# A spectral mixing layer and a feed-forward part on one Trainium2 core: turns of the interleaved transform from 6 to 5.5 half steps, and the short form of `w_out` from two tiles sooner

## The chip, the cores and the metric

The kernel runs on one core of one Trainium2 chip. The metric is the device time of one launch in microseconds (us); before the change its median is 2561.6 us. The engines are named as in the profile: PE (matrix products; PEld its weight loads), DVE (vector engine), ACT (scalar engine), POOL (GpSimd), SP (here only a queue that issues transfers).

## The reference

```python
def _attn_ref(x, w_r, w_i, b_r, b_i):              # x: 8 x 3008 x 256
    X = np.fft.rfft(x, axis=1)
    Yr = X.real @ w_r - X.imag @ w_i + b_r
    Yi = X.real @ w_i + X.imag @ w_r + b_i
    Yr = np.sign(Yr) * np.maximum(np.abs(Yr) - 0.01, 0.0)      # Yi likewise
    return np.fft.irfft(Yr + 1j * Yi, n=x.shape[1], axis=1)

def _moe_ref(x, w_in, w_out):                      # x: 24064 x 256, d_ff 2048
    r = np.maximum(x @ w_in, 0.0)
    return (r * r) @ w_out
```

The second function is applied to the output of the first. All is float32.

## The kernel before, in words

**Two streams of work.** The transform of a batch (forward stages, a complex mix with soft shrinkage, backward stages) is split into many small jobs. The feed-forward part goes over 48 tiles of tokens, six for each of the 8 batches, 504 or 500 tokens wide, each seen as two halves of h = 252 or 250 columns (the first two tiles of a batch have 252, the other four 250). A tile has 8 steps `n`, one for each 256 of the 2048 hidden units. A step has two half steps.

**A step on PE.** `Step.first` issues 12 products `psh` with `w_in`, `Step.second` the other 9: the 2x2 block product is done by seven block products instead of eight, each in three terms (high x high, low x high, high x low) that together keep float32 accuracy from fp32r operands. The operands are the tile's tokens and five sums of them (`Tokens`: B11, B21, B22, T1, T3, T2, T4), each in a high half `yt0` (an ACT cast) and a low half `yt1` (a POOL subtraction). The fourth product of a step, `S2 T2`, needs `T2`, which is made of the last columns of the tile. DVE adds the products up and rectifies them into `mc`; ACT squares `mc` and casts it to the high half `mg0`; POOL subtracts to get the low half `mg1`. Two steps later `Step.out` issues 12 matmuls `pso` of 2h columns with `w_out`.

**The short form.** In the steps `SEVEN = (1, 2, 4, 5)` of the tiles in `FREE` (line 61, tiles 38 to 46), `out_seven` (lines 809 to 832) does `w_out` by seven block products as well: 21 matmuls of h columns in place of 12 of 2h. It needs four sums of weight blocks (`out_sums`, made once when the transform is over and its memory free), and on the side of the data `cast_early` (788 to 793: the fourth block's halves `mh`, `ml`) and `forms` (795 to 807: sums `ftt` on DVE, high halves `fth` on ACT, low halves `ftl` on POOL). Its extra accumulators are joined per tile by `tile_sums` on DVE.

**What sets the order.** The main loop (1155 to 1187) goes over half steps; before each half step ends it calls the jobs whose time in half steps has come. The transform of batch b+1 is cut in 13 turns of `PACE` = 6 half steps (lines 60, 898 to 909, 1133 to 1141). Each tile's columns come from two or three inverse transforms `Back` (`back_tasks`, 911 to 935), which are loaded through one buffer `du`, transformed on PE with `dx` in groups of three matmuls into `psf`, copied by ACT (`dy`) and added by DVE into `yr`; then `Tokens.sums` (POOL `ms`) and `Tokens.split` follow. For the last two batches all inverse transforms are made ahead, in `kept_tasks` (948 to 960), once the last batch's mixing is done: two at a time are loaded (`load_two`), and their results `dy` go to memory. They begin at half step `done + 0.6`, where `done` is where the last pairs end, and tiles 36 and on read their tokens back (`raw_load`). Within these calls the framework fixes the order of each engine's instructions when the kernel is built; on the chip every engine follows its list in order, and SP issues its transfers in order.

**The tiles in FREE** take their tokens one piece at a time at steps 0, 6 and 7 (`Tokens.free`), put between the casts, so that POOL's list is written out by hand there.

## Time and profile before

| | us |
|---|---|
| median of 3 runs (2561.59 to 2561.8) | 2561.6 |
| the profiled execution | 2562.7 |
| its span | 2560.9 |
| PE busy | 2551.0 |
| DVE busy | 1875.5 |
| POOL busy | 1782.0 |
| ACT busy | 1452.5 |

The span is the time from the first to the last instruction in the trace; the profiled execution's own time is 1.8 us longer and 1.1 us above the median. PE's granted clock is 1.00 of full speed all over. An engine's busy time counts neither its waits nor the issuing of transfers. In the order of the run: a front part to about 160 us, the turns to about 1950 us, the kept transforms to about 2145 us (the start of tile 38), and from there the short steps.

### The profile page before, as it was taken

To read this page: it belongs to the slowest core of one execution; us is meant where nothing else is said; L and a number is where in the kernel's file an instruction comes from. 1 tells how busy PE (TensorE), PEld (TensorE's weight loads), DVE (VectorE), ACT (ScalarE), POOL (GpSimd) and SP (SyncE) were. 2 spreads that over 40 slices of the span, in tenths; PEclk is the share of its full clock that TensorE was granted. 3 is DMA by queue.
4 is the path that set the end of the run, shared out by engine and by line. 5 is a ranking of instruction groups with operands and counts; after the bars stand their busy time and mean duration, and the time that the engine had idled before them with its cause. 6 is when DMAs were issued, how large, how long until landed. Compare 5 with 4: busy or idle time off the path is not lost.

```text
span 2560.9 us, 48190 instructions
## 1 busy us (share of the span) xinstructions
PE 2551.0 (100%) x17534; PEld 2365.2 (92%) x17534; DVE 1875.5 (73%) x3714; ACT 1452.5 (57%) x2338; POOL 1782.0 (70%) x1804
## 2 busy tenths in 40 slices
PE   9999999999999999999999999999999999999999
PEld 7899999999999999999999999999999999999998
DVE  7876776777777777777677777777776656888885
ACT  5655555555555555555555555555555555666664
POOL 1167666776767777666676766766566857999995
PEclk9999999999999999999999999999999999999999
DMA  9633432333334333343333343332333452101000
GB/s 312 196 94 92 115 93 85 95 111 106 104 108 119 106 102 97 116 121 112 92 104 112 106 122 100 108 112 89 108 111 95 126 151 62 33 21 33 13 17 17
DMA packets 191203, 257.05 MB, mean 100 GB/s; under 512 B 18216, under 2 KB 138016, under 8 KB 190968
## 3 DMA queue, kind: packets, MB, share of 16 engines
q1 hardware_dynamic: 177553, 228.71, 28.9%
q0 software_dynamic: 13280, 25.16, 4.1%
q8 instruction: 140, 2.29, 0.4%
q14 instruction: 95, 0.78, 0.1%
q10 hardware_dynamic: 135, 0.12, 0.0%
HBM read 150.36 MB, written 103.55 MB: 99 GB/s over the span
## 4 chain that ended last, share of the span: by engine, by line
PE 97%; DVE 1%; DMA 1%; POOL 0%; ACT 0%; issue 0%; SPq 0%; DVEq 0%; ACTq 0%
PE pso L594 38%; PE psh L594 36%; PE psf L312 7%; PE psf L291 3%; PE psf L345 2%; PE psf L253 2%; PE psf L594 2%; PE psf L477 1%; PE psf L558 1%; PE psf L559 1%; PE psf L555 1%; PE psf L375 1%; PE psf L532 1%; DMA x<-x_in 0%; PE psf L487 0%; PE psf L463 0%
## 5 line engine op out<-in xcount | busy, mean ns | idle before, releaser
L115 POOL TENSOR_TENSOR mg<-mc,mg 128x500 fp32r<-128x500 f32 (+3 forms) x766 | 967.6, 1285 | 386.7 <-ACT mg L111 295.4
L594 PE MATMUL pso<-mg,wout 128*128 128x500 f32 (+2 forms) x4284 | 1080.1, 388 | 0.0
L594 PE MATMUL psh<-yt,win 128*128 128x250 f32 (+1 forms) x8064 | 1073.4, 280 | 0.8 <-DVE mc L594 0.3
L594 PEld LDWEIGHTS psh<-yt,win 128*128 128x128 f32 x8064 | 1017.7, 189 | 27.0 <-DVE yt L115 0.6
L594 PEld LDWEIGHTS pso<-mg,wout 128*128 128x128 f32 x4284 | 766.4, 188 | 120.5
L594 DVE CUSTOM_DVE_ANT_0 mc<-psh,mv 128x250 f32<-128x250 f32 (+3 forms) x769 | 418.3, 546 | 282.5 <-PE psh L594 241.7
L594 ACT ACTIVATE mc<-mc 128x1000 f32<-128x1000 f32 (+4 forms) x420 | 407.9, 971 | 342.6 <-DVE mc L594 340.4
L111 ACT CAST mg<-mc 128x1000 fp32r<-128x1000 f32 (+2 forms) x385 | 381.8, 992 | 13.9
L594 DVE TENSOR_TENSOR mv<-psh,mu 128x500 f32<-128x500 f32 (+1 forms) x384 | 260.8, 679 | 47.2 <-PE psh L594 13.3
L312 PE MATMUL psf<-wx,kxh 128*128 128x256 f32 x1008 | 210.9, 281 | 0.0
L333 DVE TENSOR_TENSOR kv<-psf,ke 64x256 f32<-64x256 f32 x336 | 141.8, 422 | 56.1 <-PE psf L312 42.1
L312 PEld LDWEIGHTS psf<-wx,kxh 128*128 128x128 f32 x1008 | 167.5, 189 | 2.7 <-DVE ke L324 0.2
L111 ACT COPY dy<-psf 128x188 f32<-128x188 f32 (+2 forms) x229 | 70.8, 315 | 167.2 <-PE psf L559 166.7
L224 POOL TENSOR_TENSOR xs<-xt 120x256 f32<-120x256 f32 x156 | 120.7, 795 | 60.1 <-DMA xt<-x_in 21.1
L112 DVE COPY mp<-psh 128x250 f32<-128x250 f32 (+1 forms) x304 | 126.6, 416 | 46.5 <-PE psh L594 31.7
L115 POOL TENSOR_TENSOR ksl<-kv,ksh 128x512 fp32r<-128x512 f32 x84 | 109.8, 1307 | 66.6 <-ACT ksh L111 59.8
L312 PE MATMUL psf<-wx,kxl 128*128 128x256 f32 x504 | 141.5, 281 | 0.0
L594 DVE TENSOR_TENSOR mu<-psh,mp 128x250 f32<-128x250 f32 (+1 forms) x304 | 127.2, 418 | 9.5
L594 DVE CUSTOM_DVE_ANT_0 mc<-psh,mp 128x250 f32<-128x250 f32 (+1 forms) x304 | 124.2, 408 | 4.8 <-PE psh L594 4.7
L115 POOL TENSOR_TENSOR yt<-yr,yt 128x250 fp32r<-128x250 f32 (+1 forms) x94 | 88.6, 944 | 43.6 <-ACT yt L111 43.1
L115 POOL TENSOR_TENSOR ftl<-ftt,fth 128x250 fp32r<-128x250 f32 (+1 forms) x144 | 107.5, 772 | 7.3 <-ACT fth L111 2.5
L335 ACT ACTIVATE kc<-kv,low 128x512 f32<-128x512 f32 x84 | 60.8, 724 | 88.4 <-DVE kv L333 88.3
(182 smaller groups left out, 3311.1 us busy)
## 6 DMA issues: line engine op xcount, KB each, us to landing
ka<-s SPq DMA_DIRECT2D x96, 256.0 KB, 3.0
du<-s SPq DMA_DIRECT2D x86, 256.0 KB, 2.9
kcm<-cm_in POOLq DMA_DIRECT2D x84, 256.0 KB, 3.7
s<-kuh SPq DMA_DIRECT2D x84, 256.0 KB, 3.2
s<-kul SPq DMA_DIRECT2D x84, 256.0 KB, 3.7
s<-xe SPq DMA_DIRECT2D x82, 240.0 KB, 2.4
xt<-x_in SPq DMA_DIRECT2D x81, 240.0 KB, 3.2
out<-mo SPq DMA_DIRECT2D x64, 250.0 KB, 2.3
```

Of the source, the lines that this page charges most:

```text
L111: return act.copy(out=out, in_=in_)
L112: return eng.tensor_copy(out=out, in_=in_)
L115: return eng.tensor_tensor(out=out, in0=a, in1=b, op=ALU.subtract)
L224: return eng.tensor_tensor(out=out[:, :n], in0=self.xt[:, :n, 0], in1=self.xt[:, :n, 1], op=(ALU.add, ALU.subtract)[t])
L253: nc.tensor.matmul(ps[:, t], am_sb[0][:, j, t], v[:, t], start=n == 0, stop=n == 2)
L291: nc.tensor.matmul(pv[:, :, c, g, :], self.a[:, g, c * 128:(c + 1) * 128], bg, start=True, stop=True)
L312: self.last = nc.tensor.matmul(ps, l, wx[j][:, k, c, :], start=n == 0, stop=n == 5)
L333: dve.tensor_add(out=v[64 * r:64 * r + 64, g], in0=ps[gs], in1=self.e[gs, r])
L335: act.activation(r, v, AF.Relu, bias=low)
L345: nc.tensor.matmul(ps[:, g], self.cm[:, g, j * 128:(j + 1) * 128], r[:, g], start=n == 0, stop=n == 2)
L375: self.mm = nc.tensor.matmul(ps[:M1, t], nam if t and i else am32[:, t], self.xt[:, 0, i], start=i == 0, stop=i == 1)
L594: last_of[eng] = op(*args, **kwargs)
```

## The change

It does five things.

- `PACE` is 5.5, so the last pairs end and the kept transforms begin 33 half steps earlier: `done` goes from half step 554.25 to 521.25, from tile 34 to tile 32. The weight sums `out_sums` move with it.
- `FREE` is tiles 35 to 47; tile 35 has short steps 4 and 5, tile 47 steps 1, 2 and 4 (`SOME`), the others all four. That is 49 short steps in place of 36; the new ones are five with h = 250 (tiles 35, 47) and eight with h = 252 (tiles 36, 37).
- `cast_early` hands its POOL subtraction `ml` back, and `forms` issues it between its two halves.
- Tile 36 makes its tokens in the way of the tiles before, three half steps sooner, and reads its raw columns sooner.
- The last tile joins its short sums one step sooner, and its output leaves through DVE additions in place of ACT's copies and DVE's.

```diff
-TURN0, TURNS, PACE = 92, J, 6
-FREE = range(ENDS * len(HALF) + 2, B * len(HALF) - 1)
+TURN0, TURNS, PACE = 92, J, 5.5
+FREE = range(ENDS * len(HALF) - 1, B * len(HALF))
...
+SOME = {FREE[0]: SEVEN[2:], FREE[-1]: SEVEN[:3]}
...
-            self.sevens = SEVEN if t in FREE else ()
+            self.sevens = SOME.get(t, SEVEN) if t in FREE else ()
...
-            then(pool, sub, pool, lo, c, hi)
+            return lambda: then(pool, sub, pool, lo, c, hi)
...
-        def forms(self):
+        def forms(self, between):
...
                     then(pool, sub, pool, self.tl[:, i], s[:, i], self.th[:, i])
+                if between:
+                    between()
+                    between = None
...
-        if t > FREE[0]:
-            return [(start - NF + (6.0 if t == FREE[0] + 1 else 4.0), lambda: raw_load(t))]
+        if t > FREE[0] + 1:
+            return [(start - NF + (6.0 if t == FREE[0] + 2 else 4.0), lambda: raw_load(t))]
...
-            jobs += [(start + 2.5, lambda: raw_load(t))]
+            jobs += [(start + (2.5 if t <= FREE[0] else 0.0), lambda: raw_load(t))]
         k = Tokens(t)
+        if t == FREE[0] + 1:
+            start -= 3.0
...
-                if steps[n].seven:
-                    steps[n].cast_early()
+                low = steps[n].seven and steps[n].cast_early()
                 if steps[n - 1].seven:
-                    steps[n - 1].forms()
-                if i == NF // 2 - 1 and t in FREE:
+                    steps[n - 1].forms(low)
+                elif low:
+                    low()
+                if i == (NF // 2 - 1 if t < FREE[-1] else NF // 2 - 2):
                     tile_sums(t)
```

**PE at the start of tile 34, before.** `psh` with `yt0`, `yt1` are the tile's products (three terms of the first product B11, then three of `S2 T2`), `psf` the transform's matmuls.

```order
L594 MATMUL psh0_25181<-yt0_24900,win0_83 128x250 [waits DVE_49]
L594 MATMUL psh0_25181<-yt0_24900,win1_84 128x250
L594 MATMUL psh0_25181<-yt1_24901,win0_83 128x250
L594 MATMUL psh0_25181<-yt0_24900,win0_83 128x250 [waits Activation_49]
L594 MATMUL psh0_25181<-yt0_24900,win1_84 128x250
L345 MATMUL psf_24945<-ksh_24823,kcm_24783 128x256 [waits DMASW7_49,PE_49,Activation_49]
...
L312 MATMUL psf_25025<-wx0_81,kxh_24865 128x256 [waits DVE_49]
...
L594 MATMUL psh0_25181<-yt1_24901,win0_83 128x250 [waits Pool_49]
```

**PE at the start of tile 34, after the change.** `psf<-dx_sb,du` are groups of three matmuls of inverse transforms; `du_25090` is the third `Back` of tile 34 itself, the other `du` are kept ones.

```order
L595 MATMUL psh0_25575<-yt0_25316,win0_83 128x250 [waits DVE_49,Activation_49]
L595 MATMUL psh0_25575<-yt0_25316,win1_84 128x250
L595 MATMUL psh0_25575<-yt1_25317,win0_83 128x250 [waits Pool_49]
L556 MATMUL psf_25167<-dx_sb_79,du_24989 128x2x94 [waits DVE_49]
...
L556 MATMUL psf_25180<-dx_sb_79,du_25090 128x2x94 [waits DMAHW2_49,DVE_49]
...
L556 MATMUL psf_25187<-dx_sb_79,du_25090 128x2x94 [waits DVE_49]
...
L556 MATMUL psf_25471<-dx_sb_79,du_25364 128x2x94 [waits DVE_49]
L559 MATMUL psf_25471<-dx_sb_79,du_25364 128x2x94
L560 MATMUL psf_25471<-dx_sb_79,du_25365 128x188
L595 MATMUL psh0_25575<-yt0_25316,win0_83 128x250 [waits Activation_49]
L595 MATMUL psh0_25575<-yt0_25316,win1_84 128x250
```

Between the third product and the fourth stand 42 transform matmuls, in 14 groups, and six more before the low term of the fourth; before it was none and eight, and the third `Back` of tile 34 stood in step 6 of tile 33.

**POOL around the tokens of tile 34, before.** `ms` are the sums of tokens, `yt1` the low halves of the tokens; `mg1_24978` belongs to step 5 of tile 33, `mg1_25067` to step 6.

```order
L115 TENSOR_TENSOR ms_24827<-yr_24413 128x250 [waits DMAHW7_49,DMAHW5_49,DVE_49]
L115 TENSOR_TENSOR ms_24827<-yr_24413 128x250 [waits DVE_49]
L115 TENSOR_TENSOR mg1_24978<-mc_24915,mg0_24977 128x500 [waits PE_49,Activation_49]
L115 TENSOR_TENSOR mg1_24978<-mc_24915,mg0_24977 128x500
L115 TENSOR_TENSOR yt1_24901<-yr_24413,yt0_24900 128x500 [waits Activation_49]
L638 TENSOR_TENSOR ms_24827<-yr_24413,ms_24827 128x250 [waits Pool_49]
L115 TENSOR_TENSOR yt1_24901<-ms_24827,yt0_24900 128x500 [waits Activation_49]
L115 TENSOR_TENSOR ms_24827<-yr_24413,ms_24827 128x250 [waits Pool_49]
L115 TENSOR_TENSOR mg1_25067<-mc_25000,mg0_25066 128x500 [waits DVE_49,Activation_49]
```

**The same after the change**; `mg1_25459` belongs to step 6 of tile 33, `mg1_25554` to step 7, the last.

```order
L116 TENSOR_TENSOR mg1_25459<-mc_25415,mg0_25458 128x500 [waits DVE_49,Activation_49]
...
L116 TENSOR_TENSOR mg1_25554<-mc_25491,mg0_25553 128x500 [waits DVE_49,Activation_49]
L116 TENSOR_TENSOR mg1_25554<-mc_25491,mg0_25553 128x500
L116 TENSOR_TENSOR ms_25231<-yr_24850 128x250 [waits DMAHW7_49,DMAHW0_49,DVE_49]
L116 TENSOR_TENSOR ms_25231<-yr_24850 128x250 [waits DVE_49]
L116 TENSOR_TENSOR yt1_25317<-yr_24850,yt0_25316 128x500 [waits Activation_49]
L639 TENSOR_TENSOR ms_25231<-yr_24850,ms_25231 128x250 [waits Pool_49]
L116 TENSOR_TENSOR yt1_25317<-ms_25231,yt0_25316 128x500 [waits Activation_49]
L116 TENSOR_TENSOR ms_25231<-yr_24850,ms_25231 128x250 [waits Pool_49]
L588 COPY yr_25559<-dy_25179 128x2x124 [waits DVE_49,Pool_49]
L116 TENSOR_TENSOR yt1_25317<-ms_25231,yt0_25316 128x500 [waits Activation_49]
```

The sums now stand behind the low half of the last step of tile 33.

**POOL in two short steps, before.** `ml` is the low half of the fourth block, `ftl` those of the sums.

```order
L115 TENSOR_TENSOR ml_28236<-mc_28208,mh_28235 128x250 [waits Activation_49]
L115 TENSOR_TENSOR mg1_28292<-mc_28208,mg0_28291 128x250 [waits DVE_49,Activation_49]
L115 TENSOR_TENSOR mg1_28292<-mc_28208,mg0_28291 128x250
L115 TENSOR_TENSOR ml_28298<-mc_28274,mh_28297 128x250 [waits Activation_49]
L115 TENSOR_TENSOR ftl_28304<-ftt_28302,fth_28303 128x250 [waits Activation_49]
L115 TENSOR_TENSOR ftl_28304<-ftt_28302,fth_28303 128x250
L115 TENSOR_TENSOR ftl_28304<-ftt_28302,fth_28303 128x250 [waits Activation_49]
L115 TENSOR_TENSOR ftl_28304<-ftt_28302,fth_28303 128x250 [waits DVE_49]
```

**The same after the change:**

```order
L116 TENSOR_TENSOR ml_28733<-mc_28709,mh_28732 128x250 [waits Activation_49]
L116 TENSOR_TENSOR mg1_28794<-mc_28709,mg0_28793 128x250 [waits DVE_49,Activation_49]
L116 TENSOR_TENSOR mg1_28794<-mc_28709,mg0_28793 128x250
L116 TENSOR_TENSOR ftl_28805<-ftt_28803,fth_28804 128x250 [waits PE_49,Activation_49]
L116 TENSOR_TENSOR ftl_28805<-ftt_28803,fth_28804 128x250
L116 TENSOR_TENSOR ml_28800<-mc_28776,mh_28799 128x250
L116 TENSOR_TENSOR ftl_28805<-ftt_28803,fth_28804 128x250 [waits Activation_49]
L116 TENSOR_TENSOR ftl_28805<-ftt_28803,fth_28804 128x250 [waits DVE_49]
```

The second `ml` stands behind the first two `ftl`.

## Rows read from the trace of the kernel before

**Rows 1.** The page: busy time and share per engine; the chain that ended last.

```profile
PE 2551.0 (100%) x17534; PEld 2365.2 (92%) x17534; DVE 1875.5 (73%) x3714; ACT 1452.5 (57%) x2338; POOL 1782.0 (70%) x1804
...
PE 97%; DVE 1%; DMA 1%; POOL 0%; ACT 0%; issue 0%; SPq 0%; DVEq 0%; ACTq 0%
```

**Rows 2.** PE's waits: waiting line, releaser, us in total, times, longest.

```profile
PE pso L594 <- POOL ftl L115: 0.6, 2, 0.3
...
PE psh L594 <- DVE yt L115: 0.2, 1, 0.2
```

**Rows 3.** Windows: us, then busy PE, PEld, DVE, ACT, POOL; clock, DMA.

```profile
163.00:386.30 223.30, 223.30 (x1557) 208.29 (x1556) 157.09 (x305) 125.82 (x190) 153.20 (x154) 1.00 0.35 101
...
2144.80:2509.20 364.40, 363.81 (x2703) 345.89 (x2702) 301.99 (x517) 235.68 (x398) 343.51 (x396) 1.00 0.07 23
```

**Rows 4.** Timeline of PE, tile 41: start, duration, engine, line, operation, tile, count.

```profile
2293.14 2.90 PE L594 MATMUL pso<-mg,wout 128*128 128x500 f32 x12
2295.88 2.62 PE L594 MATMUL psh<-yt,win 128*128 128x250 f32 x21
2298.33 0.28 PE L594 MATMUL psf<-mg,wout 128*128 128x250 f32 x1
...
2300.78 0.39 PE L594 MATMUL psh<-yt,win 128*128 128x250 f32 x2
```

**Rows 5.** Timeline of DVE in tiles 40 and 41, of POOL and PE in 41.

```profile
2238.63 1.07 DVE L115 TENSOR_TENSOR ftt<-mc 128x500 f32<-128x500 f32 x1
...
2278.87 2.91 DVE L115 TENSOR_TENSOR ftt<-mc 128x500 f32<-128x500 f32 x1
...
2278.65 0.65 POOL L115 TENSOR_TENSOR ml<-mc,mh 128x250 fp32r<-128x250 f32 x1
2279.23 1.43 POOL L115 TENSOR_TENSOR mg<-mc,mg 128x250 fp32r<-128x250 f32 x2
...
2282.50 2.83 POOL L115 TENSOR_TENSOR ftl<-ftt,fth 128x250 fp32r<-128x250 f32 x4 [1.26 <-ACT fth L111]
...
2282.47 0.28 PE L594 MATMUL psf<-mg,wout 128*128 128x250 f32 x1
...
2285.60 2.61 PE L594 MATMUL psh<-yt,win 128*128 128x250 f32 x21
2288.05 0.28 PE L594 MATMUL psf<-mg,wout 128*128 128x250 f32 x1
...
2290.69 0.51 PE L594 MATMUL psh<-yt,win 128*128 128x250 f32 x3
```

**Rows 6.** Timeline of PE and ACT at the end of tile 33; the group of `dy`.

```profile
1948.50 0.41 PE L594 MATMUL psh<-yt,win 128*128 128x250 f32 x2
...
1949.50 1.04 ACT L594 ACTIVATE mc<-mc 128x1000 f32<-128x1000 f32 x1 [0.85 <-DVE mc L594]
1950.57 1.03 ACT L111 CAST mg<-mc 128x1000 fp32r<-128x1000 f32 x1
...
L111 ACT COPY dy<-psf 128x188 f32<-128x188 f32 x224 | 69.1, 314 | 167.2 <-PE psf L559 166.7
```

**Rows 7.** Timeline of PE, POOL and ACT: tile 34's tokens, from its last transform group.

```profile
1937.51 0.28 PE L559 MATMUL psf<-dx_sb,du 128*128 128x188 f32 x1
...
1939.09 1.31 POOL L115 TENSOR_TENSOR ms<-yr 128x250 f32<-128x250 f32 x2 [2.96 <-DVE yr L568]
1940.35 2.49 POOL L115 TENSOR_TENSOR mg<-mc,mg 128x500 fp32r<-128x500 f32 x2
1942.80 1.07 POOL L115 TENSOR_TENSOR yt<-yr,yt 128x500 fp32r<-128x500 f32 x1
...
1945.44 0.73 POOL L115 TENSOR_TENSOR ms<-yr,ms 128x250 f32<-128x250 f32 x1
...
1946.62 0.61 ACT L111 CAST yt<-ms 128x500 fp32r<-128x500 f32 x1
```

**Rows 8.** Timeline of PE: two transform groups of a kept transform, and what follows.

```profile
2036.01 0.25 PE L555 MATMUL psf<-dx_sb,du 128*128 128x188 f32 x1
...
2036.65 0.64 PE L594 MATMUL pso<-mg,wout 128*128 128x500 f32 x2
```

**Rows 9.** Timeline of POOL: the copy of columns for the next tile.

```profile
1949.75 0.40 POOL L587 COPY yr<-dy 128x248 f32<-128x248 f32 x1
```

**Rows 10.** The page, transfers: tile, queue, count, size, median us to landing.

```profile
du<-s SPq DMA_DIRECT2D x86, 256.0 KB, 2.9
```

**Rows 11.** Timeline of DVE: its last instruction.

```profile
2556.67 0.42 DVE L112 COPY mo<-pso 128x250 f32<-128x250 f32 x1 [2.76 <-ACT mo L111]
```

More of the change, by code (lines that the diff above doesn't have):

```diff
@@ L830, in out_seven @@
                         pe, pe.matmul, ps, a[x], b[y][:, k],
-                        start=begins and q == at == 0, stop=i == len(SEVEN) - 1 and q == 2 and j == 1 and at in (1, 2),
+                        start=begins and q == at == 0, stop=n == self.sevens[-1] and q == 2 and j == 1 and at in (1, 2),
                     )
@@ L903, in fwd_tasks @@
             if b > 2 and q == 0:
-                add = lambda f=f, s=steps[(start - 4) // 2 - 1]: later(s.low, f.add)
+                add = lambda f=f, s=steps[int(start - 4) // 2 - 1]: later(s.low, f.add)
             elif b == 2 and q > 3:
@@ L938, in raw_load @@
         b, c0, h = tiles[t]
-        if t > FREE[0] and t % 2:
+        if t > FREE[0] + 1 and t % 2:
             raw[t] = [T(f"yr{c}", [128, 2 * HM], F32, tag="xt") for c in range(2)]
@@ L945, in raw_load @@
             load_next(y[:, :, :2 * h], ys[b][:, :, c0:c0 + 2 * h])
-            raw[t] = y if t <= FREE[0] else [y[:, c] for c in range(2)]
+            raw[t] = y if t <= FREE[0] + 1 else [y[:, c] for c in range(2)]
     def kept_tasks(ahead, start, step):
@@ L1161, in fnet_moe @@
             t, i = divmod(n - 1, NF // 2)
-            if not k and n < len(steps) and t >= FREE[0] - 1:
+            if not k and n < len(steps) and t >= FREE[0]:
                 next = t + 1 if i == 0 else t + 2
-                ahead = i in (0, 6, 7) and FREE[0] < next < len(tiles)
+                ahead = i in (0, 6, 7) and FREE[0] + 1 < next < len(tiles)
                 if ahead:
@@ L1168, in fnet_moe @@
                     tokens.free(i, False)
-                if t >= FREE[0]:
-                    steps[n - 1].casts()
+                steps[n - 1].casts()
                 if ahead:
                     tokens.free(i, True)
-                if steps[n].seven:
-                    steps[n].cast_early()
+                low = steps[n].seven and steps[n].cast_early()
                 if steps[n - 1].seven:
-                    steps[n - 1].forms()
-                if i == NF // 2 - 1 and t in FREE:
+                    steps[n - 1].forms(low)
+                elif low:
+                    low()
+                if i == (NF // 2 - 1 if t < FREE[-1] else NF // 2 - 2):
                     tile_sums(t)
```

## The prediction

> **What bounds the kernel now.** I first read the busy line and the chain that ended last [rows 1]: TensorE (PE) is busy for 2551.0 of 2560.9 us and holds 97% of the chain. The reader is to see that only two things can change the time: what PE has to do, and what makes it wait. The list of waits comes second [rows 2]: those of the feed-forward part that the change touches are two of 0.3 us, for the low halves of the fourfold sums (POOL's `ftl`), and one of 0.2 us for the low half of a tile's tokens (`yt`). The windows by stage come third [rows 3]: in the stage of batch 1, whose pairs already run at 5.25 half steps, PE is busy 223.30 of 223.30 us, so turns of 5.5 need not starve it by their number alone; in the short stage POOL is busy 343.51 of 364.4 us and is next. Last I read single stretches, and beside them where the changed order puts the same work. A difference of 0.2%, 5.1 us, is about what a measurement of this kernel can tell from no change.
>
> **Shorter steps.** A step's ordinary `w_out` is 12 matmuls of 500 columns, 2293.14 to 2295.88, 2.74 us; its short form is 21 matmuls of 250, 2298.33 to 2300.78, 2.45 us [rows 4]. Each step that changes form saves 0.29 us of PE; at 252 columns I take the same, both forms being 0.8% wider. The list of short steps grows from 36 to 49: two in tile 35, four each in 36 and 37, three in 47. 13 x 0.29 = **3.8 us less PE work**, nearly all on the chain. The turns themselves remove no PE work; they only bring the kept transforms forward, so that the sums of `w_out` are there two tiles sooner.
>
> **A delay that comes along.** A first short step lasts 2.45 us where its operands are there, but in tile 41 it starts at 2282.47 and the next products at 2285.60: 3.13 us, and the second takes 2288.05 to 2290.69, 2.64 us [rows 5]. Together 0.9 us too much. The reason stands on DVE: the first difference of the form (`ftt`, 128x500) lasts 2.91 us beside POOL's unbroken subtractions, where the same one lasts 1.07 us at 2238.63 [rows 5]; `ftl` starts only at 2282.50 [rows 5]. This befalls the tiles that prepare a 252-wide tile during short steps, 41 and 42. After the change tile 36 is a twin of 42. I add **0.9 us** for it. The new place of `ml` (between the two halves of `ftl`) leaves POOL the same instructions before the last `ftl`, so I cost it at nothing; the end below is that it dissolves all three delays, 2.7 us. The Trainium skill has a rule here, on the page "SBUF — State Buffer", section "Who interferes with whom": the port pair that VectorE and GpSimd share goes to whichever started first, for that whole instruction, and the other waits. By it DVE would wait for the rest of one POOL instruction, none of the three tiles would lose anything, and the sum would be 0.9 us lower. The trace differs: 2.91 us outlasts `mg` x2 with its 1.43 us [rows 5], so the measurement decides.
>
> **Tile 34's tokens.** This is the term that turns the sum. The columns of tile 34 come from three inverse transforms (`Back`) through one `du` buffer, their loads in SP's queue. The faster turns start the kept transforms while these still run. In the new order the third `Back` of tile 34, `du_25090`, stands on PE behind the first three products of tile 34, no longer in step 6 of the tile before; and 14 groups of three transform matmuls stand between the third product and the fourth, which needs `T2`, a sum over the last columns. What follows from that I work out by hand from rows, t = 0 at the end of tile 33's products:
> - ACT: before, the last two products of step 33.7 went out from 1948.50, so PE was through them at 1948.74; the square of that step began 0.76 us later, at 1949.50, and its cast 1.07 us after the square [rows 6]. With one `dy` copy of 0.31 us [rows 6] now between the two, and 1.03 us of its own, the cast ends at 3.2.
> - POOL: two `mg` of that step, 2.5 us [rows 7], to 5.7. Only then stand the two `ms`, 1.31 us, to 7.0, and `yt`, `ms`, `yt`, `ms`, which went from 1942.80 to 1945.44 + 0.73, 3.37 us [rows 7], to 10.4.
> - ACT casts `T2` in 0.61 us [rows 7]: 11.0.
> - PE until then: three products, 0.35 us by [rows 4] (21 in 2.45), and 14 groups; two groups took 2036.01 to 2036.65 [rows 8], 0.32 each, 4.5 in all. That is 4.8 us of work.
> PE then waits 6.2 us. Behind it the low half of `T2` (POOL's copy, 0.4 by [rows 9], and 1.07 us [rows 7]) is ready at 12.5, while PE has two products and two more groups, 0.9 us, to 11.9: 0.6 more, of which I take nothing, the copy being mostly done beside ACT's cast. **6.2 us.** Everything else on PE is queued behind these products: the outputs of 33.6 and 33.7 too. The lower end comes if POOL's `mg` were done early: from the group at 1937.51 to the end of the last `ms` at 1946.17 the trace has 8.4 us with 2.5 us of `mg` in it [rows 7]; the third `Back` at 1.6, plus 5.9, plus 0.6 is 8.1, a wait of 3.3. The upper end comes if the load is late: it is issued when `du_24985` is read, some 6.8 us of PE work before its use, behind a kept load three times as large; one load lands in 2.9 us [rows 10], so I allow 2 us of lateness, 8.2.
>
> **Tile 31.** Its third `Back` is late by less: its second group stands in step 30.6. From there PE has some 10 us of work to the high half of `T2`: 33 products at 0.117 us and 12 output matmuls [rows 4], 3.85 and 2.74, and some 30 transform matmuls at about 0.11 [rows 8], 3.3. The same chain took 1937.8 to 1947.2, 9.4 us, in [rows 7], and now has two more `mg` before `T2`, 2.5 us. So 11.9 against 10: I take **1.5 us**, ends 0 and 3, the upper since 22 more transform matmuls that depend on one another stand before its low half. Tile 13 has 21 such matmuls between the halves; ends 0 and 1, taken as 0.
>
> **The rest.** The sooner tokens of tile 36, the tile sums one step sooner in the last tile and the deferred `ml` move a few instructions of DVE, POOL and ACT, each beside PE's work: DVE is busy 301.99 of 364.4 us there [rows 3]; if that cover is short somewhere, one `ml` of 0.65 us [rows 5] is what can come late. At the end two DVE additions take the place of ACT's copies and DVE's 0.42 us copy [rows 11]; between 0.1 less and 0.2 more, taken as 0.
>
> **Sum.** -3.8 + 0.9 + 6.2 + 1.5 = +4.8 us. Against the profiled execution, 2562.7, that is 2567.5; the median of the runs shown stands 1.1 us lower, 2561.6, so **2566.4 us**.
>
> **Rivals.**
> 1. *The waits at the tile starts are short.* The matmuls pulled ahead cover the token chain, as they do in the trace of before, where all tile starts together cost PE 0.2 us for `yt` [rows 2]. Against it: there no more than eight stood between the third product and the sixth of tile 34, and its third `Back` was done a step and a half before. Then 2561.6 - 3.8 + 0.9 = 2558.7 us, faster than before though within 0.2%. It decides from the point where `T2` is cast within 4.8 us of tile 34's start.
> 2. *The same, and the new place of `ml` ends the delays of 41, 42 and 36*: 2561.6 - 3.8 - 1.8 = 2556.0 us, faster by over 0.2%. For it: POOL's run beside `ftt` is one instruction shorter, 0.65 us. Against it: the same POOL work still precedes the last `ftl`.
> 3. *Only the least wait*: 3.3 at tile 34 and 0 at tile 31, 2562.0 us.
> 4. *The denser turns cost more than the two places*: `mg`, which PE's outputs need, is often queued on POOL behind transform work, and 65 turns give room for many waits of 0.1 us. For it: the same crowding of the order at tiles 13, 22 and 24. Against it: the stage at 5.25 without a wait [rows 3]. With 3 to 5 us more, some 2570 us.
>
> **How the numbers follow.** Forecast 0.45 (own range 2563 to 2569), rival 1 0.2, rival 2 0.1, rival 3 0.13, rival 4 0.12. Faster by over 0.2% (below 2556.5) is rival 2 and a bit of rival 1: 0.13. Slower by over 0.2% (above 2566.7) is rival 4 and over half of the forecast's upper part, since tile 34's wait may be 8.2: 0.37. The rest, 0.5, lies within. The range reaches from the edge of rival 2 to rival 4: 2556.5 to 2570.5.
>
> **What would show it.** Right: in the profile after, PE's waits name ACT `yt` and POOL `yt` with a longest of some 6 us, at the start of tile 34, near 1950 us; tile 34 is longer than the 52 us it had by nearly that; short steps of tiles 35 to 37 and 47 take 2.45 us; tile 36's first takes about 3.1. Wrong: no wait above 1 us in the transform stage (rival 1), a first `ftt` of about 1.1 us in tiles 36, 41 and 42 (rival 2), or many waits of PE for `mg` all over the turns (rival 4).

## The result, and the profile after

The change makes the kernel **slower: 2587.6 us** (median of 4 runs, 2584.7 to 2588.9) against 2561.6 before, a ratio of 1.010 with a 95% interval of 1.0088 to 1.0113. The forecast was 2566.4 in a range of 2556.5 to 2570.5: the sign was right, the size was not, 26 us against 4.8. The profiled execution has a span of 2586.4 us, 25.5 more than before. Two launches of the experiments below were disturbed (4169.8 and 14452.9 us) and are left out of their medians.

The page of the kernel after, busy times and the chain that ended last:

```profile
PE 2560.4 (99%) x17651; PEld 2376.9 (92%) x17651; DVE 1896.0 (73%) x3752; ACT 1473.3 (57%) x2406; POOL 1808.8 (70%) x1869
...
PE 95%; DVE 2%; DMA 1%; ACT 1%; issue 0%; POOL 0%; SPq 0%; DVEq 0%; ACTq 0%
```

Against [rows 1] PE's share of the chain has fallen from 97% to 95%: PE waits now. A busy time of PE that is 9.4 us longer, with less work to do, is the other sign; the clock, below, explains part of it. The waits of PE in the kernel after:

```profile
PE psf L313 <- DVE kp L303: 2.8, 3, 1.4
PE psh L595 <- DVE mu L595: 2.2, 2, 2.0
PE psf L560 <- DMA du<-s: 1.8, 1, 1.8
PE psf L556 <- DVE dy L563: 1.5, 5, 0.6
PE psf L346 <- DVE mc L595: 1.3, 1, 1.3
...
PE psf L313 <- DVE kv L334: 1.1, 1, 1.1
...
PE psf L556 <- DVE ke L325: 0.8, 1, 0.8
...
PE pso L595 <- POOL ftl L116: 0.3, 1, 0.3
PE psh L595 <- DVE yt L116: 0.2, 1, 0.2
```

A row gives the us in total, how often, and the longest. The transform's `psf`, which in the kernel before waits in the front part alone, to 163 us, now heads the list, and most of it waits for DVE (`kp`, `kv`, `ke` and `dy` belong to the transform, `mu` and `mc` to the steps). No wait for a tile's tokens, `yt`, is long, not even at tile 34.

To place the loss I took, for every matmul, the time to the start of the next less the median of that time for its number of columns, and added these up by tile. This counts a wait and a slowed clock alike. Against before there are 19.6 us more in tiles 1 to 33 (most of them in tiles 18, 31, 27, 13 and 17: 6.2, 3.3, 3.2, 2.2 and 1.7 us, in the others 1.2 or less) and 11.1 us in tile 34, and 1.1 us less in the front part and from tile 35 on. Less the 3.8 us of work that the short form saves, that is +25.8, near the 25.5 of the spans.

**Tile 34** first. Its start in the kernel after, PE, then POOL and ACT:

```profile
1985.08 0.35 PE L556 MATMUL psf<-dx_sb,du 128*128 128x188 f32 x1 [0.46 <-DVE dy L563]
...
1986.22 0.36 PE L556 MATMUL psf<-dx_sb,du 128*128 128x188 f32 x1 [0.57 <-DVE dy L563]
...
1987.48 0.49 PE L556 MATMUL psf<-dx_sb,du 128*128 128x188 f32 x1 [0.68 <-ACT dy L112]
1987.77 0.42 PE L559 MATMUL psf<-dx_sb,du 128*128 128x188 f32 x1
1987.98 0.42 PE L560 MATMUL psf<-dx_sb,du 128*128 128x188 f32 x1
...
1994.90 0.49 PE L556 MATMUL psf<-dx_sb,du 128*128 128x188 f32 x1 [0.62 <-DMA du<-s]
...
1997.36 0.53 PE L560 MATMUL psf<-dx_sb,du 128*128 128x188 f32 x1 [1.75 <-DMA du<-s]
...
1998.32 0.68 PE L595 MATMUL psh<-yt,win 128*128 128x250 f32 x2
...
1986.78 2.45 POOL L116 TENSOR_TENSOR mg<-mc,mg 128x500 fp32r<-128x500 f32 x2 [3.20 <-ACT mg L112]
1989.19 1.30 POOL L116 TENSOR_TENSOR ms<-yr 128x250 f32<-128x250 f32 x2
...
1993.10 0.71 POOL L116 TENSOR_TENSOR ms<-yr,ms 128x250 f32<-128x250 f32 x1
...
1994.53 0.61 ACT L112 CAST yt<-ms 128x500 fp32r<-128x500 f32 x1
```

The products of tile 33 end at 1983.46 in the trace. `T2` is cast at 1995.14, 11.7 us later; the prediction's hand chain gave 11.0. But PE asks for `T2` only at 1998.32, 3.2 us after that, and does not wait for it. The 14 groups between, which the prediction took for 4.5 us of work that covers part of a wait, take 14.5 us, from 1983.81 until then: their columns arrive late (two waits for `du<-s`), most pairs of groups wait for their banks to be emptied (the waits for `dy`), and from 1987.5 on PE issues a matmul of 188 columns every 0.21 us, where in [rows 8] it was 0.11. The windows of the kernel after, with the granted clock in the column before the last two:

```profile
1983.00:1990.00 7.00, 5.14 (x31) 4.43 (x30) 3.16 (x10) 4.07 (x9) 3.80 (x5) 0.81 0.57 166
1990.00:2000.00 10.00, 7.32 (x30) 6.40 (x30) 2.83 (x8) 3.79 (x11) 5.26 (x7) 0.50 0.79 236
2000.00:2010.00 10.00, 10.00 (x64) 9.19 (x64) 6.72 (x16) 3.61 (x8) 1.01 (x1) 0.95 0.59 176
```

A granted clock of 0.50 is the lower of TensorE's two levels, 1.2 of 2.4 GHz. It came after the first waits of this place (0.46, 0.57 and 0.68 us between 1984.5 and 1987.5) and was at full speed again soon after 2000. So these waits cost more than their own length: what PE did next was slow as well, and counts as busy. Not every wait does that: with 0.8, 1.1 and 0.3 us at the start of tile 31 the granted clock stayed at 1.00.

**The short steps** save what was forecast. Tile 36's, in the kernel after:

```profile
2108.53 0.28 PE L595 MATMUL psf<-mg,wout 128*128 128x252 f32 x1
...
2111.23 2.59 PE L595 MATMUL psh<-yt,win 128*128 128x252 f32 x21
2113.66 0.28 PE L595 MATMUL psf<-mg,wout 128*128 128x252 f32 x1
...
2116.16 0.52 PE L595 MATMUL psh<-yt,win 128*128 128x252 f32 x3
```

The first takes 2.70 us and the second 2.50, together 0.3 over the 2.44 us each that 21 such matmuls need, not the 0.9 of tile 41 in [rows 5]. The first `ftt` of tile 36 takes 1.26 us, not 2.91.

### The profile page after: what moved, and what is told of

It is laid out like the page before. It is cut to its first block, busy times and chain, and to the rows that moved or that the text cites. A ratio compares the mean times of both kernels' runs of the same rounds, so it can differ in the third digit from the quotient of the medians.

```text
span 2586.4 us, 48565 instructions
## 1 busy us (share of the span) xinstructions
PE 2560.4 (99%) x17651; PEld 2376.9 (92%) x17651; DVE 1896.0 (73%) x3752; ACT 1473.3 (57%) x2406; POOL 1808.8 (70%) x1869
## 4 chain that ended last, share of the span: by engine, by line
PE 95%; DVE 2%; DMA 1%; ACT 1%; issue 0%; POOL 0%; SPq 0%; DVEq 0%; ACTq 0%
PE pso L595 37%; PE psh L595 36%; PE psf L313 7%; PE psf L292 3%; PE psf L595 3%; PE psf L346 2%; PE psf L254 2%; PE psf L478 1%; PE psf L560 1%; PE psf L559 1%; PE psf L556 1%; PE psf L376 1%; PE psf L533 1%; PE psf L413 0%; PE psf L488 0%
## 5 line engine op out<-in xcount | busy, mean ns | idle before, releaser
L116 POOL TENSOR_TENSOR mg<-mc,mg 128x500 fp32r<-128x500 f32 (+3 forms) x766 | 949.3, 1260 | 384.4 <-ACT mg L112 297.6
L595 PE MATMUL pso<-mg,wout 128*128 128x500 f32 (+3 forms) x4167 | 1050.2, 387 | 0.0
L595 PEld LDWEIGHTS pso<-mg,wout 128*128 128x128 f32 x4167 | 747.8, 189 | 116.2
L595 ACT ACTIVATE mc<-mc 128x1000 f32<-128x1000 f32 (+5 forms) x433 | 410.5, 948 | 297.8 <-DVE mc L595 295.4
L112 ACT CAST mg<-mc 128x1000 fp32r<-128x1000 f32 (+3 forms) x385 | 376.2, 977 | 14.9
L116 POOL TENSOR_TENSOR ftl<-ftt,fth 128x250 fp32r<-128x250 f32 (+1 forms) x196 | 147.4, 773 | 9.9 <-ACT fth L112 1.3
L113 DVE COPY mp<-psh 128x250 f32<-128x250 f32 (+1 forms) x280 | 116.4, 416 | 39.4 <-PE psh L595 28.1
L595 DVE TENSOR_TENSOR mu<-psh,mp 128x250 f32<-128x250 f32 (+1 forms) x280 | 117.0, 418 | 8.1
L595 DVE CUSTOM_DVE_ANT_0 mc<-psh,mp 128x250 f32<-128x250 f32 (+1 forms) x280 | 114.8, 410 | 6.4 <-PE psh L595 5.7
L112 ACT CAST fth<-ftt 128x500 fp32r<-128x500 f32 (+1 forms) x98 | 60.0, 613 | 92.6 <-DVE ftt L116 90.0
```

What stands on the lines that cost most here:

```text
L112: return act.copy(out=out, in_=in_)
L113: return eng.tensor_copy(out=out, in_=in_)
L116: return eng.tensor_tensor(out=out, in0=a, in1=b, op=ALU.subtract)
L595: last_of[eng] = op(*args, **kwargs)
```

## The experiments

The theory at this point had two parts: the denser turns set an order in which PE, or what PE needs, waits at a handful of places (20 us), and the kept transforms run into the inverse transforms of tile 34 (11 us). The rivals were the short form and its small changes, and the mere density of the turns. The first four runs undo one thing each.

**The turns alone**, on the kernel before:

```diff
-TURN0, TURNS, PACE = 92, J, 6
+TURN0, TURNS, PACE = 92, J, 5.5
...
```

> The kernel before with turns of 5.5 half steps and nothing else of the change. Theory (the new turns set the order of PE so that dependent transform matmuls stand too close to what they wait for, and tile 34's tokens come too late): about 2591 us, that is 18 us more in the turns (tiles 2 to 31) and about 12 us in tile 34, and no short step gained. Rival (the waits come from the longer list of short steps or from the small changes to them): within 2 us of 2561.6.

Measured 2591.7 us (ratio 1.0118, 1.0103 to 1.0133). All of the loss is here, and a little more: the rest of the change gives 4 us back.

**The rest of the change without the turns:**

```diff
-TURN0, TURNS, PACE = 92, J, 5.5
-FREE = range(ENDS * len(HALF) - 1, B * len(HALF))
+TURN0, TURNS, PACE = 92, J, 6
+FREE = range(ENDS * len(HALF) + 1, B * len(HALF))
```

> The change with turns of 6 half steps, and the short form from tile 37 on (41 short steps, 5 more than before), as the weight sums come no sooner; all the small changes kept. Theory: the turns and the start of tile 34 as before, 5 x 0.29 = 1.5 us gained by the short steps and about 1 us by the new place of ml: 2559 us. Rival (the short form or the small changes cost the time): 2570 us or more.

Measured 2559.7 us (0.9981 to 1.0): as expected, though the interval touches no change.

**The kept transforms at their old time**, with the turns alone:

```diff
-    jobs += [(done + 0.5, late)] + kept_tasks(over + 6.0, done + 0.6, 1.4)
+    jobs += [(done + 0.5, late)] + kept_tasks(over + 6.0, done + 33.6, 1.4)
```

> Turns of 5.5 half steps, nothing else of the change, but the kept transforms begin at the half step at which they began before (33 later than in the changed kernel). Theory (tile 34's loss comes from the kept transforms that run into its own inverse transforms): tile 34 takes some 52 to 54 us again in place of 64, and the time is about 2579 us, the 18 us of the turns remaining. Rival (tile 34 is late because the turns are dense): as with the turns alone, about 2591 us.

Measured 2580.8 us (1.006 to 1.009). Tile 34 takes 44.7 us and loses nothing; it is shorter than expected, since only 31 transform matmuls stand in it, against 108 with the turns alone. PE in the windows around tile 34 and after it, in this kernel:

```profile
1939.00:1990.00 51.00, 51.00 (x335) 46.65 (x334) 30.42 (x68) 27.55 (x41) 44.48 (x51) 1.00 0.23 69
1990.00:2040.00 50.00, 50.00 (x330) 45.77 (x329) 29.62 (x66) 25.66 (x38) 29.94 (x28) 1.00 0.29 90
```

PE is busy without a gap. So 11 us of the loss are the collision, and 19 remain in the turns.

**The same density, all turns one half step later**, on the kernel before:

```diff
-TURN0, TURNS, PACE = 92, J, 6
+TURN0, TURNS, PACE = 93, J, 6
```

> The kernel before with turns of 6 half steps as before, but all of them one half step later (first turn at 93 in place of 92). Same density of transform work. Theory (what counts is where a turn's work falls against the tile's): waits of 4 to 10 us at the start of tile 34, where this order puts 32 transform matmuls between the third and the fourth product and a matmul right behind what it depends on, and no other wait above 1 us: about 2567 us. Rival (it is the density of the turns that costs): no difference, 2561.6 us within 1.

Measured 2573.2 us (1.003 to 1.0063), more than expected, most of it at the place expected: tile 34 loses 7.4 us, tiles 1 to 33 another 3.2 in pieces of under 1 us. PE's longest waits there:

```profile
1955.31 0.38 PE L312 MATMUL psf<-wx,kxh 128*128 128x256 f32 x1 [1.65 <-ACT kxh L111]
1956.75 0.38 PE L312 MATMUL psf<-wx,kxl 128*128 128x256 f32 x1 [1.05 <-DVE kxl L115]
```

The density is that of the kernel before, which loses next to nothing there. The old pair of numbers, 92 and 6, is a fit to the tiles.

**Two more pacings** to part order from density. I had counted, in each new order, the PE work between the matmuls that make a pair's operands and the first product of its mix; where it was under 3.5 us, the changed kernel had lost time.

```diff
-TURN0, TURNS, PACE = 92, J, 6
+TURN0, TURNS, PACE = 93, J, 5.5
...
```

> Turns of 5.5 half steps as in the run with the turns alone, but all one half step later (first at 93); nothing else of the change. The density is the same. In this order only two places (near the start of tile 32 and in tile 10) have less than 3 us of PE work between the first product of a pair's mix and the matmuls that make its operands, against five places with the first turn at 92; at the start of tile 34 31 transform matmuls stand before the fourth product, against 42. Theory (the order of the places decides): waits of 4 to 6 us in the turns in place of 18, about 9 in tile 34: 2572 to 2578 us. Rival (density decides): as with the turns alone, 2589 to 2593.

Measured 2593.3 us (1.0105 to 1.0142): just above the rival's window.

```diff
-TURN0, TURNS, PACE = 92, J, 6
+TURN0, TURNS, PACE = 92, J, 5.75
...
```

> The kernel before with turns of 5.75 half steps, halfway, and nothing else of the change. In this order no mix stands within 3.5 us of PE work of its operands' matmuls, and 9 transform matmuls stand before the fourth product of tile 34. Theory (order decides): 2562 to 2566 us. Rival (density decides, in proportion): half of the 30 us, about 2576 us.

Measured 2585.8 us (1.0082 to 1.0109): more than either expected. By tiles, 13.5 us of its loss stand in tile 34 and 10 to 12 in tiles 1 to 33; with turns of 5.5 from 93 on it was 12.8 in tile 34, and in tiles 1 to 33 the places were others (tile 10 5.8 us, tile 14 3.2). So my count does not tell where time is lost: it saw one link of a chain of many. PE's longest waits with turns of 5.75:

```profile
PE psf L555 <- DMA du<-s: 4.7, 1, 4.7
PE psf L253 <- DVE xl L115: 2.4, 1, 2.4
PE psf L345 <- ACT ksh L111: 2.3, 1, 2.3
```

The second line led on: `xl`, the low half of a turn's input.

**The new place of `ml`**, a possible gain of its own, on the kernel before:

```diff
-            then(pool, sub, pool, lo, c, hi)
+            return lambda: then(pool, sub, pool, lo, c, hi)
...
+                if between:
+                    between()
+                    between = None
...
```

> The kernel before with the POOL subtraction of the fourth block (ml) placed between the two halves of the forms, nothing else. By the prediction (no effect): 2561.6 us and 41.2 and 41.4 us for tiles 41 and 42. By the trace of the changed kernel (first short steps of tiles 36 and 42 without delay): 1 us less, 2560.7 us, tile 42 at about 40.6 and tile 41 about as before.

Measured 2561.0 us against 2561.5 (0.9989 to 1.0007): the interval holds no change. In the trace tile 42 takes 40.63 us and tile 41 41.04, where it was 41.41 and 41.22. But tile 42 takes 40.59 us with the turns alone as well, where `ml` has its old place and the first `ftt` of the tile lasts 1.26 us, so this is not shown to be the work of `ml`.

**Turns of 5.75 with the short form from tile 36:**

```diff
-TURN0, TURNS, PACE = 92, J, 5.5
-FREE = range(ENDS * len(HALF) - 1, B * len(HALF))
+TURN0, TURNS, PACE = 92, J, 5.75
+FREE = range(ENDS * len(HALF), B * len(HALF))
```

> The change with turns of 5.75 half steps and the short form from tile 36 on (45 short steps). Theory: the turns as with 5.75 alone, less 9 x 0.29 = 2.6 us for the short steps and about 1 us for ml: 2558 to 2562 us, so at best a little below the run with turns of 6 and 41 short steps (2559.7). Rival (density): 2572 us.

Measured 2584.6 us (1.0074 to 1.0101): a miss that goes with that of 5.75 alone; the nine more short steps give 1.2 us, where 2.6 were expected.

**Which half of the turns, and why.** A new theory: DVE makes `xl` at a place in its list that is tied to the steps' own instructions; when `xl` waits, the next step's additions wait behind it, and PE behind them. First the two kinds of turn apart, both with batches of the old length, so that nothing later moves:

```diff
-            f, even = Fwd(b, q), start + PACE * q
+            f, even = Fwd(b, q), start + 5.5 * q
```

> The kernel before; the 13 forward turns of a batch follow each other by 5.5 half steps, but a batch still takes 78 half steps and its pairs (mix and back transform) keep their 6, so nothing later moves. Theory A (the forward turns and their xl on DVE make the waits): most of the 19 us that the turns lost, 2573 to 2581 us. Theory C (the pairs' chain of mix, shrink and back transform makes them): 2561 to 2566 us. Theory B (both together, by density): about half, 2568 to 2573 us.

Measured 2581.4 us (1.0057 to 1.0087): 19 us, theory A, 0.4 above its window.

```diff
-        jobs += pair_tasks(pairs[b], start + PACE + 1.0, PACE if b < B - 1 else 5.25)
+        jobs += pair_tasks(pairs[b], start + PACE + 1.0, 5.5 if b < B - 1 else 5.25)
```

> The kernel before; the 12 pairs of a batch follow each other by 5.5 half steps, but a batch still takes 78 half steps and its forward turns keep their 6. Theory A (forward turns): 2561 to 2566 us. Theory C (the pairs' chain): most of the 19 us, 2573 to 2581 us. Theory B (density of both): about half, 2568 to 2573 us.

Measured 2567.9 us (1.0011 to 1.003), 6 us: between A and B. The forward turns weigh most. These are orders of their own, though: with forward turns of 5.5 alone the loss stands in tiles 13, 21 and 23 (7.0, 4.2 and 4.2 us), not in 18, 31 and 27, tile 21's wait is for a load (`ka`), and 19 and 6 add up to more than the 19 of both. How `xl` makes PE wait is seen in the run with forward turns of 5.5, in tile 13 (DVE, ACT, SP's queue, PE):

```profile
819.19 0.69 DVE L115 TENSOR_TENSOR xl<-xs,xh 120x512 fp32r<-120x512 f32 x1 [4.52 <-DMA s<-xe]
819.80 0.41 DVE L112 COPY mp<-psh 128x252 f32<-128x252 f32 x1
...
821.88 0.42 DVE L594 TENSOR_TENSOR mu<-psh,mp 128x252 f32<-128x252 f32 x1
...
814.79 0.58 ACT L111 COPY xe<-psf 120x512 f32<-120x512 f32 x1
815.47 0.62 ACT L111 CAST xh<-xs 120x512 fp32r<-120x512 f32 x1
...
815.40 0.34 SPq L234 DMA_DIRECT2D s<-xe  x1
...
822.36 0.97 PE L594 MATMUL psh<-yt,win 128*128 128x252 f32 x4 [2.68 <-DVE mu L594]
```

`xh`, which `xl` needs, is there at 816.1. DVE, idle from 814.67, stands still for 4.52 us all the same, to 819.19, until the store of `xe`, issued at 815.40, has ended: the input of a turn, its fold `xs`, its halves `xh` and `xl` and its result `xe` pass through one ring of three buffers, and `xl` gets the one in which the result of the turn before still lies. Behind `xl` stand `mp` and `mu` of the next step, and PE waits 2.68 us for `mu`.

**`xl` free of its place**, on the run with the kept transforms held back (2580.8 us):

```diff
-            then(dve, sub, dve, self.l, self.u, self.h)
+            sub(dve, self.l, self.u, self.h)
```

> As the run with turns of 5.5 half steps and the kept transforms at their old time (2580.8 us, of which about 19 us in the turns, none in tile 34), but DVE's subtraction xl, the low half of a turn's input, is no longer tied to its place in DVE's list of the steps' own instructions. Theory A (in the turns PE waits because xl waits for its input at a fixed place in DVE's list, with the next step's own additions behind it): most of the 19 us go, 2565 to 2571 us. Theory B (xl is only one of many links that come too near; with denser turns the next link takes its place): 2575 to 2582 us.

Measured 2573.2 us (1.0026 to 1.0055): 7.6 of 19 us, between the two. In its trace the losses of tiles 18, 27, 13 and 17 are gone (6.2, 3.2, 1.6 and 1.6 us less than in the run without this edit); tile 31's 3.3 us stay, and some 1 us each has come up in tiles 5, 6 and 10. Then **a fourth buffer**, on the same base:

```diff
-    zero = const.tile([128, 128], F32, name="warm")
+    zero = const.tile([128, 16], F32, name="warm")
...
-            how(pe, pe.matmul, ps[:, :128], zero, zero, start=True, stop=True)
+            how(pe, pe.matmul, ps[:16, :128].rearrange("p (a b) -> p a b", a=8), zero, zero.unsqueeze(1).broadcast_to([128, 8, 16]), start=True, stop=True)
...
-    "xt": 3, "xe": 1, "du": 1, "kv": 1, "kp": 1, "kq": 1, "ksh": 1, "ksl": 1, "kxl": 1, "kuh": 1, "kul": 1, "kb": 1, "yr": 1,
+    "xt": 4, "xe": 1, "du": 1, "kv": 1, "kp": 1, "kq": 1, "ksh": 1, "ksl": 1, "kxl": 1, "kuh": 1, "kul": 1, "kb": 1, "yr": 1,
...
-    nam = T("nam", [M1, M1], F32)
+    nam = T("nam", [M1, M1], F32, tag="xt")
```

> As the run with turns of 5.5 half steps and the kept transforms at their old time (2580.8 us, about 19 us lost in the turns), with four buffers in place of three in the ring through which a turn's input, its fold, both halves and its result pass (room for it: the zeros of the warm-up matmuls are kept once in 16 columns and read broadcast, and a small matrix of the first tiles lies in the ring). The order of the engines' instructions stays the same but for a few rows. Theory (xl, at its fixed place on DVE, waits until the result of the turn before has been stored and its buffer is free): DVE's idle time before xl that ends with that store, about 13 us, goes, and the time falls by 6 to 12 us, to 2569 to 2575. Rival (the buffer is not what counts; xl waits for the cast xh just as long): 2578 to 2583 us.

Measured 2569.9 us (1.0021 to 1.005). The control, the same edits with three buffers:

> Turns of 5.5 half steps, kept transforms at their old time, zeros and small matrix as in the run with four buffers, but three buffers. If the ring's third buffer is what holds xl: 2578 to 2583 us, the 11 us of the fourth buffer gone, with DVE's idle time before xl by the store of xe back at about 13 us. If the other two edits (or the places in memory) gave them: 2568 to 2573 us.

Measured 2577.2 us (1.0046 to 1.0078), just under the window of the first theory. So by the medians the edits that made room gave 3.6 of the 10.9 us, and the buffer 7.3. The control's four runs lie far apart, 2574.4 to 2583.8, so that the split is not sharp; but the lowest of them is above the highest with four buffers, 2572.7. DVE's group `xl` (count, busy us and mean ns, idle time before it and what ended that), in the kernel before,

```profile
L115 DVE TENSOR_TENSOR xl<-xs,xh 120x512 fp32r<-120x512 f32 x78 | 90.4, 1159 | 8.2 <-ACT xh L111 8.2
```

in the changed kernel,

```profile
L116 DVE TENSOR_TENSOR xl<-xs,xh 120x512 fp32r<-120x512 f32 x78 | 90.6, 1161 | 23.1 <-DMA s<-xe 12.8 <-ACT xh L112 8.4 <-ACT kxh L112 1.9
```

with the turns alone and the kept transforms held back,

```profile
L115 DVE TENSOR_TENSOR xl<-xs,xh 120x512 fp32r<-120x512 f32 x78 | 87.9, 1127 | 23.7 <-DMA s<-xe 13.2 <-ACT xh L111 8.5 <-ACT kxh L111 2.0
```

in the control,

```profile
L115 DVE TENSOR_TENSOR xl<-xs,xh 120x512 fp32r<-120x512 f32 x78 | 88.0, 1128 | 24.2 <-DMA s<-xe 13.0 <-ACT xh L111 8.6 <-ACT kxh L111 2.6
```

and with four buffers:

```profile
L115 DVE TENSOR_TENSOR xl<-xs,xh 120x512 fp32r<-120x512 f32 x78 | 83.0, 1064 | 14.0 <-ACT xh L111 14.0
```

The kernel before has no idle time there that ends with a store of `xe`. The 13 us of it that come with turns of 5.5 are gone with the fourth buffer, and with it alone: with `xl` free of its place 14.8 us of it stand there, and hold up less. What is left waits for `xh`.

**Both cures together:**

> Turns of 5.5 half steps, kept transforms at their old time, four buffers and xl free of its place in DVE's list. Each alone gave back 8 (free) and 11 us (four buffers) of 19. If both cure the same wait: as with four buffers, 2568 to 2571 us. If they cure different waits: 2561 to 2565 us.

Measured 2563.2 us (0.9998 to 1.0016). They add up: 17.6 us together, 18.5 apart, so beside the store `xl` also waited at its fixed place for something else, by the group above for `xh`. The time cannot be told from that of the kernel before, but turns of 5.5 are not free: the two edits that made room are in this run, and below they gain 5 us with turns of 6. Against turns of 6 with these edits and four buffers (2554.8 us below, of which five more short steps gain 1.5) some 7 us remain by this estimate, about 3 of them at tile 31's start.

**The fourth buffer in the whole change:**

> The whole change with four buffers in the turns' ring. If the shares found apart add up in the changed kernel itself: 2587.6 less the 11 us that the fourth buffer gave back with the turns alone, 2575 to 2578 us, with 10 to 13 us still lost at the start of tile 34. If the wait at tile 34 takes up what the turns give back: 2583 us or more.

Measured 2579.2 us (1.0053 to 1.0081), 8.5 us less than the change, a little short of the 11 expected. No run has the whole change with the two edits and three buffers, so the buffer's share of this is not known apart. Tile 34 still loses 11.2 us in its trace: the two losses are separate.

**At the old turn length**, with 41 short steps:

> Turns of 6 half steps, short form from tile 37 on (the run with 41 short steps, 2559.7 us), with four buffers. In the turns of 6 PE waits for nothing, so the fourth buffer should give nothing: 2558.5 to 2560.5 us. If the lean turns hide small waits: 2556 or less.

Measured 2554.8 us (0.9962 to 0.9983): a surprise, 4.9 us less than the same kernel without the buffer, in which PE waits for next to nothing. Its control, with three buffers:

> As the run with turns of 6 half steps, 41 short steps and four buffers (2554.8 us), but with three buffers again; the zeros in 16 columns and the small matrix in the ring stay. If the fourth buffer gave the 4.9 us against the run with 41 short steps alone (2559.7): 2559 to 2560. If they come from where the buffers lie in memory, since in the trace every kind of matmul is issued 0.3 to 2 ns sooner on the mean, in tiles without turns too: another value, in steps of 1 to 5 us from 2559.7 to either side.

Measured **2554.6 us** (0.996 to 0.9983), so the buffer gives nothing there, as expected, and the two small edits give it all. This version beats both kernels, by 7.0 us and by 33. The groups of products in the run with 41 short steps (count, busy us, mean ns),

```profile
L595 PE MATMUL psh<-yt,win 128*128 128x250 f32 x5376 | 712.4, 280 | 0.0
L595 PE MATMUL pso<-mg,wout 128*128 128x500 f32 x2700 | 678.3, 391 | 0.0
```

and with the two edits:

```profile
L595 PE MATMUL psh<-yt,win 128*128 128x250 f32 x5376 | 709.4, 279 | 0.0
L595 PE MATMUL pso<-mg,wout 128*128 128x500 f32 x2700 | 675.3, 390 | 0.0
```

The same matmuls in the same order take 3 us less in each of these two groups. No wait is removed; these matmuls follow each other sooner by 0.6 and 1.1 ns on the mean, those of 252 columns later by 0.4 ns. The gain stands in the odd tiles of 250 columns, 0.3 to 0.5 us in 14 of 16, also where no turns are (tile 39 takes 40.07 us, not 40.34); most other tiles are the same within 0.2 us, and tiles 41 and 42 are 0.6 longer. Beside the warm-up matmuls at the front, what differs is where in the memory the kernel's buffers lie. That this is the cause is the nearest reading, and was not tested by itself.

## Why the prediction was right in its sign and wrong in its size

- **Less work in short steps, -3.8 us: right.** The steps of tile 36 show it, and the whole change takes 4.0 us less than its turns alone.
- **Tile 36's delay, +0.9: too large.** It was 0.3 us there, and tile 42's delay went nearly away: the long `ftt` did not come. Why it comes or not stays open; where it came, in [rows 5], it ended at 2281.78, 1.12 us after the last of POOL's `mg` x2 (2280.66), about the 1.07 us that it takes elsewhere, as if it had waited for POOL's whole run and not for one instruction. The new place of `ml`, costed at nothing, is not shown to decide it: tile 42 takes 40.59 us in the run with the turns alone, with the old order, and 41.30 in the fastest version, with the new one. In the time the new place alone cannot be told from no change.
- **Tile 34, +6.2 (3.3 to 8.2): right place and right intruder, wrong wait; 11.1.** The chain to `T2` came out within 0.7 us, but PE never waited for `T2`; waits for `yt` with a longest of some 6 us were what the prediction named as the sign of being right. The step that failed is the cover: "14 groups; two groups took 2036.01 to 2036.65 [rows 8], 0.32 each, 4.5 in all". That is the price of a group whose columns are loaded, whose bank is free and whose clock is full. Here none of the three held, the groups took 14.5 us, and `T2` had been ready for 3.2 us when they ended. That the kept transforms are the reason is shown by holding them back.
- **Tile 31, +1.5 (0 to 3): too small; 3.3.** PE waits for no token here either, but for the transform: 0.8 us for `ke` before the fourth product, 1.1 and 0.3 for `kv` and `kxl` before its low half, where the prediction had 22 dependent matmuls as the reason for its upper end. Tile 13, taken as 0 with an end at 1, lost 2.2.
- **The rest of the turns: the step that failed most.** The prediction took it as 0, "turns of 5.5 need not starve it by their number alone", from the stage of batch 1 whose pairs run at 5.25 [rows 3], and gave rival 4, denser turns, 0.12 and "3 to 5 us more". It cost 19 us of the 26. That stage has dense pairs and not dense forward turns, and it is these that cost most: 19 us with forward turns of 5.5 alone, 6 with pairs of 5.5 alone. Also the row was a busy share of PE, which says nothing of how near to waiting DVE was. What rival 4 named as the mechanism, `mg` queued on POOL, was not it either. For some 13 of the 19 us (17.6 less the 4 to 5 of the two edits) it was DVE's `xl` at a fixed place, and a ring of three buffers.
- **The sign was right in part by luck.** The plus of the forecast hung on tile 34 alone (without it the sum is -1.4 us), where PE did not wait as forecast, and 19 of the 26 us come from a term taken as 0.
- **The reading of the order was too narrow.** I had compared how many transform matmuls stand at the starts of the tiles. Three of the five tiles that lost most, 17, 18 and 27, lost it in their steps 6 and 7.

What stays open: 3.3 us at tile 31, which stay in every run with all turns at 5.5 from 92 on; the other 3 us or so that turns of 5.5 still cost with both cures; why each of the other pacings tried loses at the start of tile 34 by a mechanism of its own (kept loads with 5.5 and 5.75, the last pairs' chain with 93 and 6); and whether it is the place in memory that makes products faster, and which.

## What to carry to other kernels

When background work is interleaved at a fixed pace, a change of the pace is a change of every order in the program; it has to be costed link by link, and for each link one asks which buffer it needs and whether that buffer's last user is a transfer. An instruction of the background that is tied to its place in a foreground list makes its own wait a wait of the foreground: free it, or give it a buffer more. And matmuls pulled ahead are a cover only when their data are there, their banks are free and the clock stays up. A small edit that makes room for a test needs a control of its own: here two such edits alone gained 5.0 us.

## What the runs showed of the hardware that was not expected

- Waits of 0.46 to 0.68 us in a row, in a stretch where PE was busy 5.14 of 7 us, were followed by ten microseconds at a granted clock of 0.50, with 0.21 us for each matmul in place of 0.11.
- Two edits that shrink a buffer of zeros and move a small matrix changed the time by 5.0 us of 2560 (2559.7 to 2554.6) with the same order of the products on PE, nearly all of it in every second tile, 0.3 to 0.5 us each. That the places of the buffers are the reason was not tested by itself.
